# Plain queries for the first batch's scores, and its inter term summed on the output's bank

## The chip, the cores and the metric

One core of one Trainium2 chip. The metric is device time in microseconds (us). TensorE is called PE here, VectorE DVE, ScalarE ACT, GpSimd POOL, and SyncE SP; SP issues almost all the transfers. The kernel was timed three times before the change, and one further execution was profiled.

## The reference

Three layers run one after the other. The first is a retention layer with 8 heads of 64 features over 2 batches of 768 tokens. The two others are MLPs from 512 to 2048 and back, the first behind a Fourier mix. In float32:

```
for b in range(nb):                                   # blocks of 64 tokens
    intra = einsum('bhic,bhjc->bhij', qb, kb) * Dmask[None]
    intra = einsum('bhij,bhjd->bhid', intra, vb)
    inter = einsum('bhid,bhde->bhie', qb * lam_pow[None], kv_state)
    out[:, :, sl] = intra + inter
    kv_state = lam_block * kv_state + einsum('bhsd,bhse->bhde', kb * rev_pow, vb)
x = out as (batch, token, 512)
u = x + real(fft(fft(x, axis=1), axis=2))
u = u + relu(layernorm(u) @ w_ch1) @ w_ch2
out = u + relu((layernorm(u) * g_ln) @ w_ch1b) @ w_ch2b
```

The change concerns `intra` and `inter` only.

## The kernel before

The retention works on chunks of 128 tokens, six to a batch. For a chunk c the kernel computes masked scores, their product with v (the output O), and an inter term from the running state of the chunks before. Float32 data that goes through fast products is split into two float16 parts, high and low, and three of the four products are summed (`PASS`). So each score tile goes DVE (mask, L324), ACT (high part, L327), POOL (low part, L329), and then PE (O, L400). The scores and the inter term themselves are float32 products on PE; one such product stands as two records in the trace.

The two batches are treated differently. Batch 0 runs alone at the start and is followed by its Fourier mix. Batch 1 runs later, between the products of the first MLP, which by then has work for PE.

In batch 0 a score product uses all 128 rows of the PE array. Two heads lie on top of each other in the 128 partitions of the key tile; the queries are loaded into rooms that have been cleared (`qz`, L184 to L189), each head's half into columns of its own (L170), so that one product of 256 columns gives two heads. Plain queries (`qt`) are loaded as well for chunks 1 to 5. In batch 1 a score product uses 64 rows and 128 columns for one head, and the code writes the two halves of the array in turn, one head of the upper and one of the lower rows (L339 to L343).

The inter term of batch 0 multiplies the plain queries by a tile that holds the state of two heads on its diagonal (`diag`, L355). DVE scales the product by the decay of each token (`lp`, L359), and then DVE adds it to the output while it reads O out of its PSUM bank (L406; L404 for chunk 0, which has no inter term). The state goes POOL (decay, L425), PE (L432), DVE (add, L439), ACT (copy to `diag`, L444).

SP issues loads in the order of the code. What comes first is lambda, the loads of chunks 0 to 5 in turn, then the first weight tiles (`ws`, L252), the Fourier tables, more weight tiles, and the first two chunks of batch 1.

The order on the other engines is set in two ways. From the start to chunk 4's inter term, and again from the first MLP on, a planner at compile time lays out each engine's queue from its own estimates. Between the two, the string `ORDER` gives the order by hand: `s` is chunk 4's state, `O4` and `O5` the outputs, `B0` and `B1` the score tiles of chunk 5, `I` its inter term, `R`, `k` and `j` the folds that start the Fourier mix, `c` steps of the first weight conversions (L269 to L273 on DVE), `W12` twelve filler products on PE. The engines execute their queues in order, whichever way the order came about.

SBUF tiles of the retention come from a pool of 13 rooms (`f`), from 8 rooms for loads (`ld`), and from rooms that weights use later (`w1_*`, `w2_*`). PSUM banks come in groups `at` (3), `dn` (3) and `up` (2); batch 0's scores use `at`, its outputs and inter products `up`.

Of the kernel before, what the change touches and what calls it, by code (L numbers as in the profile page):

```python
# [43 lines left out]
c0 B1 B1 s B0 O4 B0 O4 B0 O4 c0 B1 s s c0 R k2 j2 s k2 c0 B0 I B1 c0 I k2 O5 O5 j2 c1 k2 O5 j2 k2 W12 d24 O5  # L44
# [69 lines left out]
def tile_retention_fourier_mlp(ctx: ExitStack, tc: tile.TileContext, a: dict, out: bass.AP):  # L114
# [49 lines left out]
    def load(b, c, names=("kt", "qt", "v", "k")):  # L164
        for nm in names:
            n = ("kt", "qt", "v", "k").index(nm)
            if b == 0 and nm == "qt":
                for e in range(2):
                    r = slice(e * D, (e + 1) * D)
                    sp.dma_start(qz[c % 4][r, :, e], a[nm][b, c, r].rearrange("p (i t) -> p i t", t=P))  # L170
                if c == 0:
                    continue
            if b == 0 and c >= 2:
                t = wpool.tile([P, 512], F32, tag=f"w2_{(4 * (c - 1) + n) % 16}", name=f"{nm}{b}_{c}")
            elif b == 0 and nm == "qt":
                t = f32t(f"qt{b}_{c}")
# [7 lines left out]
    qrooms = [wpool.tile([P, 2, 4, 512], F16, tag=f"w1_{g}", name=f"qz{g}").rearrange("p a k n -> p (a k n)").bitcast(F32)  # L184
              for g in range(2)]
    qz = [qrooms[c // 2][:, c % 2 * 1024:c % 2 * 1024 + 1024].rearrange("p (i e t) -> p i e t", e=2, t=P) for c in range(4)]
    for c in range(4):
        for e in range(2):
            (dve if c % 2 == 0 else pool).memset(qz[c][(1 - e) * D:(2 - e) * D, :, e], 0.0)  # L189
# [26 lines left out]
    diag = [diag[:, i * 512:(i + 1) * 512].rearrange("p (i n) -> p i n", n=P) for i in range(2)]  # L216
    for i in range(2):
        for e in range(2):
            pool.memset(diag[i][(1 - e) * D:(2 - e) * D, :, e * D:(e + 1) * D], 0.0)
# [93 lines left out]
    def attn_x(b, c, x, bk):  # L313
        if b == 0:
            pss[x] = bank(bk["s"], f"ps_s{b}_{c}_{x}")
            for i in range(2):
                pe.matmul(pss[x][:, i * 2 * P:(i + 1) * 2 * P], loaded["kt", b, c][:, (2 * x + i) * P:(2 * x + i + 1) * P],
                          qz[c % 4][:, 2 * x + i].rearrange("p e t -> p (e t)"), start=True, stop=True)
        yield
        m32 = f32t(f"m32_{b}_{c}_{x}")  # L320
        mk = mask[:, 4 * x:4 * x + 4] if b == 0 else mask[:, x::2]
        mk = mk[:, :, :P] if c >= 3 else mk[:, :, P:0:-1]
        mo, mi = (z.rearrange("p (h i) -> p h i", i=P) for z in (m32, pss[x]))
        dve.scalar_tensor_tensor(mo, mi, MS, mk, op0=ALU.mult, op1=ALU.mult)  # L324
        yield
        t = ms[b, c, x] = hl(f"m{b}_{c}_{x}")
# [5 lines left out]
    pss = {}  # L332

    def attn_b(b, c, bk):
        steps = [attn_x(b, c, x, bk) for x in range(2)]
# [12 lines left out]

    def attn_i_steps(b, c, bk):
        t = f32t(f"int{b}_{c}")  # L350
        lp_ = lp[:, 1 if c >= 3 else 0]
        if b == 0:
            ps = bank(bk["i"], f"ps_i{b}_{c}")
            for i in range(H // 2):
                pe.matmul(ps[:, i * P:(i + 1) * P], loaded["qt", b, c][:, i * P:(i + 1) * P], diag[(c - 1) % 2][:, i],  # L355
                          start=True, stop=True)
            yield
            to, ti = (z.rearrange("p (h d) -> p h d", h=H) for z in (t, ps))
            dve.tensor_tensor(to, ti, lp_.unsqueeze(2).to_broadcast([P, H, D]), op=ALU.mult)  # L359
        else:  # L360
            for e in range(2):
                ps, r = bank(bk["i"], f"ps_i{b}_{c}_{e}"), slice(e * D, (e + 1) * D)
                for i in range(H // 2):
                    cols = slice(i * D, (i + 1) * D)
                    pe.matmul(ps[:, cols], loaded["qt", b, c][r, i * P:(i + 1) * P], states[(c - 1) % 2][r, cols], start=True, stop=True)
                to = t.rearrange("p (i e d) -> p i e d", e=2, d=D)[:, :, e]
                ti = ps[:, :H // 2 * D].rearrange("p (i d) -> p i d", d=D)
                dve.tensor_tensor(to, ti, lp_[:, e::2].unsqueeze(2).to_broadcast([P, H // 2, D]), op=ALU.mult)
        xt[b, c] = t
        yield  # L370

    def attn_i(b, c, bk):
        if c > 0:
            run(attn_i_steps(b, c, bk))
# [19 lines left out]
    def attn_o_steps(b, c, bk):  # L394
        ps = bank(bk["o"], f"ps_o{b}_{c}")
        for h in range(H):
            (x, i), hc = divmod(h, 4) if b == 0 else (h % 2, h // 2), slice(h * D, (h + 1) * D)
            m_, mc = ms[b, c, x], slice(i * P, (i + 1) * P)
            for n, (x, y) in enumerate(PASS):
                pe.matmul(ps[:, hc], m_[:, x, mc], vs[b, c][:, y, hc], start=n == 0, stop=n == 2)  # L400
        yield
        x_ = U[b][c] if c < 3 else U[b][8 - c]
        if c == 0:
# [487 lines left out]
    def eng(n):  # L891
# [4 lines left out]
              "O5": lambda: attn_o_steps(0, 5, bk0), "I": lambda: attn_i_steps(0, 5, bk0), "R": lambda: row_fold(0)}  # L896
# [172 lines left out]
```

## Time and profile before

| | us |
|---|---|
| median of 3 runs | 640.51 |
| lowest, highest | 638.93, 642.65 |
| the profiled execution | 639.05 |
| its span, first to last instruction | 637.3 |

| engine | busy us (share of the span) | instructions |
|---|---|---|
| PE | 587.2 (92%) | 4645 |
| DVE | 466.4 (73%) | 988 |
| ACT | 260.1 (41%) | 524 |
| POOL | 296.8 (47%) | 307 |

Shares are means over stages with different limits, so the stages have to be read one by one. The mean granted clock of PE is 0.976 of full speed.

### The profile page before, as it was taken

The numbers are of one execution on the slowest core, as the hardware profiler recorded it, in microseconds if no ns is written. First come the engines' busy times: TensorE is split into PE (matmuls) and PEld (weight loads), VectorE is DVE, ScalarE is ACT, GpSimd is POOL, SyncE is SP. The second block draws the span as 40 slices with busy tenths as digits, with TensorE's granted clock in tenths as the row PEclk, the third lists the DMA queues.
The fourth block names the chain that finished last, engine by engine and source line by source line (L and its number), as shares of the span: only waits on it lengthen the run. The fifth ranks groups of instructions, "written<-read, shape, count | busy, mean of one in ns | idle before, by whom it ended". The sixth has DMA issues, their size and how long they took to land.

```text
span 637.3 us, 11878 instructions
## 1 busy us (share of the span) xinstructions
PE 587.2 (92%) x4645; PEld 386.3 (61%) x4645; DVE 466.4 (73%) x988; ACT 260.1 (41%) x524; POOL 296.8 (47%) x307
## 2 busy tenths in 40 slices
PE   5857969899999999889999986899999999999997
PEld 3753734556654455466777654665767676767773
DVE  6999797898698847975579999998653643464343
ACT  3643556664432342342228755565233213321110
POOL 6856748877546555651118986696211101120000
PEclk9969799799999999999999999999999999999999
DMA  9994126986300001011016743482010014102001
GB/s 247 304 382 162 43 68 163 241 264 209 100 1 1 1 18 34 0 26 26 2 34 182 195 138 102 149 203 62 17 51 17 17 57 61 34 2 72 29 1 49
DMA packets 47139, 59.96 MB, mean 94 GB/s; under 512 B 26095, under 2 KB 31084, under 8 KB 47084
## 3 DMA queue, kind: packets, MB, share of 16 engines
q1 hardware_dynamic: 46412, 59.13, 32.5%
q8 instruction: 36, 0.59, 0.4%
q10 hardware_dynamic: 672, 0.08, 0.1%
q14 instruction: 19, 0.16, 0.1%
HBM read 50.55 MB, written 4.72 MB: 87 GB/s over the span
## 4 chain that ended last, share of the span: by engine, by line
PE 55%; DVE 27%; DMA 8%; issue 4%; POOL 2%; ACT 2%; SPq 1%; DVEq 0%; ACTq 0%; POOLq 0%
PE ps_y L811 25%; PE ps L764 18%; PE ps_h L674 5%; DVE wf L273 3%; DVE ps_w L269 3%; DVE ps_w L271 3%; DMA kt<-in_kt 2%; DMA qz<-in_qt 2%; DVE bst L608 2%; PE ps_s L343 1%; DVE tr L727 1%; DMA ws<-in_w 1%; DVE wr L707 1%; DMA cdsd<-in_cd 1%; DVE h L797 1%
## 5 line engine op out<-in xcount | busy, mean ns | idle before, releaser
L811 PE MATMUL ps_y<-w,h 128*128 128x512 f16 x1152 | 281.0, 379 | 5.7 <-DVE h L797 2.4
L811 PEld LDWEIGHTS <-h 128*128 128x128 f16 x1152 | 109.1, 98 | 108.1 <-DVE h L797 5.0
L764 PEld LDWEIGHTS <-sw 128*128 128x128 f16 x1104 | 94.5, 98 | 22.5 <-issue 8.3
L286 POOL TENSOR_TENSOR w<-wf,w 128x512 f16<-128x512 f32 x64 | 76.2, 1196 | 50.4 <-ACT w L284 50.4
L764 PE MATMUL ps<-th,sw 128*128 128x192 f16 x828 | 92.8, 246 | 6.0 <-ACT th L739 3.0
L764 PEld LDWEIGHTS <-w 128*128 128x128 f16 x828 | 71.8, 98 | 20.1 <-issue 2.9
L674 PE MATMUL ps_h<-unT,w 128*128 128x384 f16 x396 | 76.1, 336 | 7.1 <-DVE h L689 3.6
L796 ACT ACTIVATE h<-ps 128x384 f16<-128x384 f32 x92 | 43.9, 489 | 78.8 <-DVE ps L790 67.5
L764 PE MATMUL ps<-unT,w 128*128 128x192 f16 x552 | 62.6, 246 | 0.0
L674 PEld LDWEIGHTS <-w 128*128 128x128 f16 x396 | 38.4, 100 | 38.7 <-issue 7.7
L784 DVE TENSOR_TENSOR t<-ps,s 128x192 f32<-128x192 f32 x46 | 16.2, 353 | 54.2 <-PE ps L764 54.1
L740 POOL TENSOR_TENSOR th<-ts,th 128x384 f16<-128x384 f32 x28 | 25.6, 931 | 62.3 <-ACT th L739 62.1
L797 DVE SCALAR_TENSOR_TENSOR h<-ps,h 128x384 f16<-128x384 f32 x92 | 49.1, 552 | 3.9 <-ACT h L796 2.3
L719 POOL TENSOR_TENSOR sw<-ws,sw 128x512 f16<-128x512 f32 x32 | 41.2, 1298 | 21.2 <-ACT sw L718 21.2
L637 POOL TENSOR_TENSOR uns<-un,uns 128x512 f16<-128x512 f32 x21 | 24.8, 1182 | 41.7 <-ACT uns L636 41.4
L283 ACT ACTIVATE wf<-wf 128x512 f32<-128x512 f32 x48 | 30.1, 629 | 33.2 <-DVE wf L273 32.9
L776 ACT COPY s<-ps 128x192 f32<-128x192 f32 x46 | 14.5, 317 | 70.4 <-PE ps L764 70.4
L269 DVE TENSOR_SCALAR ps_w<-ws 128x512 int32<-128x512 int32 x54 | 37.0, 688 | 7.0 <-DMA ws<-in_w 6.4
L284 ACT CAST w<-wf 128x512 f16<-128x512 f32 x64 | 39.0, 615 | 1.1
L790 DVE TENSOR_TENSOR ps<-ps,s 128x192 f32<-128x192 f32 x46 | 16.6, 362 | 29.4 <-PE ps L764 29.2
L616 POOL TENSOR_TENSOR rs<-rs,neghalf 128x1 f32<-128x1 f32 x24 | 13.7, 578 | 50.8 <-DVE rs L614 50.8
L271 DVE SCALAR_TENSOR_TENSOR ps_w<-ws,ps_w 128x512 int32<-128x512 int32 x54 | 37.0, 688 | 0.4
(154 smaller groups left out, 888.9 us busy)
## 6 DMA issues: line engine op xcount, KB each, us to landing
ws<-in_w SPq DMA_DIRECT2D x25, 512.0 KB, 4.8
ws<-in_w2b SPq DMA_DIRECT2D x16, 512.0 KB, 3.4
ws<-in_w1b SPq DMA_DIRECT2D x16, 512.0 KB, 3.9
kt<-in_kt SPq DMA_DIRECT2D x12, 256.0 KB, 3.7
v<-in_v SPq DMA_DIRECT2D x12, 256.0 KB, 5.6
k<-in_k SPq DMA_DIRECT2D x12, 256.0 KB, 5.2
qt<-in_qt SPq DMA_DIRECT2D x11, 256.0 KB, 5.9
pre<-in_w SPq DMA_DIRECT2D x4, 512.0 KB, 7.4
```

What stands on the lines that cost most here:

```text
L269: dve.tensor_scalar(part, raw[:, :, 1], 3, REST, op0=ALU.logical_shift_left, op1=ALU.bitwise_and)
L271: dve.scalar_tensor_tensor(part, raw[:, :, 1], KEEP, part, op0=ALU.bitwise_and, op1=ALU.bitwise_or)
L283: act.activation(t, t, AF.Copy, scale=sc)
L284: act.copy(hi, t)
L286: (dve if m == 0 and i in (LD1 if kind == 1 else LD2) else pool).tensor_tensor(lo, t, hi, op=ALU.subtract)
L674: pe.matmul(ps, w[:, i, k, fo:fo + P], x[:, j, k, :], start=n == 0, stop=n == 11)
L719: pool.tensor_tensor(lo, z, hi, op=ALU.subtract)
L740: pool.tensor_tensor(t[:, 1], z, t[:, 0], op=ALU.subtract)
L764: pe.matmul(ps, lhs, rhs, start=start and n == 0, stop=n == 5, skip_group_check=True)
L796: act.activation(hi, z, AF.Relu)
L797: dve.scalar_tensor_tensor(lo, z, 0.0, hi, op0=ALU.max, op1=ALU.subtract)
L811: pe.matmul(dn[blk][j], h[:, x, j * P:(j + 1) * P], w[:, y], start=f == 0 and n == 0, stop=f == NF - 1 and n == 2)
```

## The change

For batch 0 the cleared query rooms go, with their 8 memsets and 12 transfers. Plain queries are loaded for all six chunks. The scores of both batches come from one code: for each half e of the array's rows, four products of 64 rows and 128 columns, first all of e = 0, then all of e = 1. Batch 1's own loop, which put the halves in turn, goes too.

For the inter term of batch 0, the decay is laid out once in the layout of the queries (`lpt`: a broadcast copy on ACT, four transposes on PE and a scaled copy on ACT, for each of two token orders). POOL multiplies the queries of chunks 1 to 5 by it (`ql`). The four products of `ql` with `diag` follow O's 24 products on O's own bank. ACT reads that bank out for all six chunks; the DVE scaling (L359) and the DVE addition (L404, L406) go from batch 0. The two `I` leave `ORDER`. Batch 1's inter term stays as it is.

```
-c0 B1 B1 s B0 O4 B0 O4 B0 O4 c0 B1 s s c0 R k2 j2 s k2 c0 B0 I B1 c0 I k2 O5 O5 j2 c1 k2 O5 j2 k2 W12 d24 O5
+c0 B1 B1 s B0 O4 B0 O4 B0 O4 c0 B1 s s c0 R k2 j2 s k2 c0 B0 B1 c0 k2 O5 O5 j2 c1 k2 O5 j2 k2 W12 d24 O5
...
-            if b == 0 and nm == "qt":
-                for e in range(2):
-                    r = slice(e * D, (e + 1) * D)
-                    sp.dma_start(qz[c % 4][r, :, e], a[nm][b, c, r].rearrange("p (i t) -> p i t", t=P))
-                if c == 0:
-                    continue
...
-    for c in range(4):
-        for e in range(2):
-            (dve if c % 2 == 0 else pool).memset(qz[c][(1 - e) * D:(2 - e) * D, :, e], 0.0)
...
+    for i in range(2):
+        wide_lp, ps = f32t(f"lpw{i}"), bank("up", f"ps_lp{i}")
+        act.copy(wide_lp.rearrange("p (h d) -> p h d", h=H), lp[:, i].unsqueeze(2).to_broadcast([P, H, D]))
+        for k in range(NK):
+            pe.transpose(ps[:, k * P:(k + 1) * P], wide_lp[:, k * P:(k + 1) * P], ident)
+        act.activation(lpt[i], ps, AF.Copy, scale=1.0 / XS)
...
+        if b == 0 and c > 0:
+            xt[b, c] = f32t(f"ql{b}_{c}")
+            pool.tensor_tensor(xt[b, c], loaded["qt", b, c], lpt[1 if c >= 3 else 0], op=ALU.mult)
...
+    def attn_x(b, c, e, bk):
+        pss = bank(bk["s"], f"ps_s{b}_{c}_{e}")
+        for i in range(H // 2):
+            r, t = slice(e * D, (e + 1) * D), slice(i * P, (i + 1) * P)
+            pe.matmul(pss[:, t], loaded["kt", b, c][r, t], loaded["qt", b, c][r, t], start=True, stop=True)
+        yield
...
-        if b > 0:
-            for e in range(2):
-                pss[e] = bank(bk["s"], f"ps_s{b}_{c}_{e}")
-            for i in range(H // 2):
-                for e in range(2):
-                    r = slice(e * D, (e + 1) * D)
-                    t = slice(i * P, (i + 1) * P)
-                    pe.matmul(pss[e][:, t], loaded["kt", b, c][r, t], loaded["qt", b, c][r, t], start=True, stop=True)
+        for z in steps:
+            next(z)
...
-            dve.tensor_tensor(to, ti, lp_.unsqueeze(2).to_broadcast([P, H, D]), op=ALU.mult)
...
+        if b == 0 and c > 0:
+            for i in range(H // 2):
+                ic = slice(i * P, (i + 1) * P)
+                pe.matmul(ps[:, ic], xt[b, c][:, ic], diag[(c - 1) % 2][:, i], start=False, stop=True, skip_group_check=True)
         yield
         x_ = U[b][c] if c < 3 else U[b][8 - c]
-        if c == 0:
+        if b == 0:
+            act.activation(x_, ps, AF.Copy, scale=XS)
+        elif c == 0:
```

## Rows read from the trace of the kernel before

**Rows 1.** Stretch, length, busy (instructions) of PE, PEld, DVE, ACT, POOL, clock, DMA share, GB/s.

```profile
8.00:16.00 8.00, 6.73 (x57) 4.51 (x55) 4.10 (x7) 3.01 (x6) 4.82 (x4) 1.00 1.09 299
16.00:24.00 8.00, 6.88 (x99) 5.60 (x99) 6.98 (x11) 6.18 (x13) 5.90 (x6) 1.00 1.11 276
24.00:33.00 9.00, 8.09 (x104) 7.00 (x105) 8.02 (x12) 5.34 (x10) 8.23 (x9) 1.00 1.07 340
33.00:44.00 11.00, 5.88 (x89) 5.21 (x88) 10.69 (x12) 4.03 (x8) 6.57 (x8) 0.67 1.02 379
44.00:64.00 20.00, 15.41 (x84) 6.72 (x81) 20.00 (x36) 8.31 (x18) 11.79 (x11) 0.84 0.56 207
136.00:200.00 64.00, 63.56 (x586) 39.95 (x585) 55.39 (x94) 29.53 (x54) 42.19 (x40) 1.00 0.33 110
```

**Rows 2.** DVE's queue in order of time: start, us, instruction, idle before.

```profile
33.01 1.30 DVE L269 TENSOR_SCALAR wf<-ws 128x512 int32<-128x512 int32 x1 [0.99 <-DMA ws<-in_w]
...
35.44 0.68 DVE L359 TENSOR_TENSOR int<-ps_i,lp 128x512 f32<-128x512 f32 x1
36.03 1.27 DVE L324 SCALAR_TENSOR_TENSOR m<-ps_s,mask 128x512 f32<-128x512 f32 x2
...
40.16 3.50 DVE L273 SCALAR_TENSOR_TENSOR wf<-ws,wf 128x512 int32<-128x512 int32 x1
43.58 0.68 DVE L463 TENSOR_TENSOR e<-u 128x512 f32<-128x512 f32 x1
```

**Rows 3.** Groups by line, first 50 us: count, busy us, mean ns, idle before.

```profile
L317 PE MATMUL ps_s<-qz,kt 128*128 128x256 f32 x48 | 14.4, 435 | 8.1 <-DMA qz<-in_qt 7.5 <-DVE m L324 0.7
...
L298 POOL TENSOR_TENSOR kd<-k,rev 128x512 f32<-128x512 f32 x5 | 5.7, 1136 | 1.4 <-DMA k<-in_k 1.3
...
L302 ACT ACTIVATE vhl<-v 128x512 f16<-128x512 f32 x6 | 3.8, 627 | 3.8 <-DMA v<-in_v 3.8
...
L406 DVE SCALAR_TENSOR_TENSOR u<-ps_o,int 128x512 f32<-128x512 f32 x5 | 3.4, 679 | 0.3 <-PE ps_o L400 0.3
L359 DVE TENSOR_TENSOR int<-ps_i,lp 128x512 f32<-128x512 f32 x5 | 3.4, 675 | 0.0
```

**Rows 4.** Transfers issued in the first 34 us: count, KB each, us to landing.

```profile
qz<-in_qt SPq DMA_DIRECT2D x12, 128.0 KB, 6.4
...
qt<-in_qt SPq DMA_DIRECT2D x5, 256.0 KB, 5.4
```

**Rows 5.** POOL's queue in order of time.

```profile
8.04 1.04 POOL L298 TENSOR_TENSOR kd<-k,rev 128x512 f32<-128x512 f32 x1
10.32 1.16 POOL L329 TENSOR_TENSOR m<-m,m 128x512 f16<-128x512 f32 x1 [1.25 <-ACT m L327]
...
40.85 2.25 POOL L329 TENSOR_TENSOR m<-m,m 128x512 f16<-128x512 f32 x2
```

**Rows 6.** PE's queue in order of time, batch 0.

```profile
25.70 1.13 PE L317 MATMUL ps_s<-qz,kt 128*128 128x256 f32 x4
26.67 0.57 PE L400 MATMUL ps_o<-vhl,m 128*128 128x64 f16 x14
27.08 1.14 PE L355 MATMUL ps_i<-diag,qt 128*128 128x128 f32 x8
...
72.76 0.60 PE L649 MATMUL ps_l<-expo,un 128*128 128x128 f32 x4
```

**Rows 7.** PE's queue in order of time, batch 1.

```profile
137.78 1.71 PE L343 MATMUL ps_s<-qt,kt 64*128 64x128 f32 x16
...
148.80 1.16 PE L343 MATMUL ps_s<-qt,kt 64*128 64x128 f32 x8
...
161.49 1.17 PE L343 MATMUL ps_s<-qt,kt 64*128 64x128 f32 x16
162.59 1.47 PE L811 MATMUL ps_y<-w,h 128*128 128x512 f16 x6
163.99 1.10 PE L365 MATMUL ps_i<-state,qt 64*128 64x64 f32 x8
```

More of the change, by code (lines that the diff above doesn't have):

```diff
@@ L183, in tile_retention_fourier_mlp @@
     U = [[ut[b][:, j] for j in range(6)] for b in range(B)]
-    qrooms = [wpool.tile([P, 2, 4, 512], F16, tag=f"w1_{g}", name=f"qz{g}").rearrange("p a k n -> p (a k n)").bitcast(F32)
-              for g in range(2)]
-    qz = [qrooms[c // 2][:, c % 2 * 1024:c % 2 * 1024 + 1024].rearrange("p (i e t) -> p i e t", e=2, t=P) for c in range(4)]
-    for c in range(4):
-        for e in range(2):
-            (dve if c % 2 == 0 else pool).memset(qz[c][(1 - e) * D:(2 - e) * D, :, e], 0.0)
     load(0, 0, ("kt", "qt"))
@@ L216, in tile_retention_fourier_mlp @@
     diag = [diag[:, i * 512:(i + 1) * 512].rearrange("p (i n) -> p i n", n=P) for i in range(2)]
+    lpt = [z.rearrange("p a k n -> p (a k n)").bitcast(F32)[:, i * 512:(i + 1) * 512]
+           for z in (wpool.tile([P, 2, 4, 512], F16, tag="w1_1", name="lpt"),) for i in range(2)]
+    for i in range(2):
[4 more added lines that the diff above has]
+        act.activation(lpt[i], ps, AF.Copy, scale=1.0 / XS)
     for i in range(2):
@@ L311, in tile_retention_fourier_mlp @@
     PASS = ((0, 0), (0, 1), (1, 0))
[L313 to L318, printed above, removed]
+    def attn_x(b, c, e, bk):
[3 more added lines that the diff above has]
+            pe.matmul(pss[:, t], loaded["kt", b, c][r, t], loaded["qt", b, c][r, t], start=True, stop=True)
         yield
-        m32 = f32t(f"m32_{b}_{c}_{x}")
-        mk = mask[:, 4 * x:4 * x + 4] if b == 0 else mask[:, x::2]
+        m32 = f32t(f"m32_{b}_{c}_{e}")
+        mk = mask[:, e::2]
         mk = mk[:, :, :P] if c >= 3 else mk[:, :, P:0:-1]
-        mo, mi = (z.rearrange("p (h i) -> p h i", i=P) for z in (m32, pss[x]))
+        mo, mi = (z.rearrange("p (h i) -> p h i", i=P) for z in (m32, pss))
         dve.scalar_tensor_tensor(mo, mi, MS, mk, op0=ALU.mult, op1=ALU.mult)
         yield
-        t = ms[b, c, x] = hl(f"m{b}_{c}_{x}")
+        t = ms[b, c, e] = hl(f"m{b}_{c}_{e}")
         act.copy(t[:, 0], m32)
@@ L330, in attn_x @@
         yield
-    pss = {}
     def attn_b(b, c, bk):
-        steps = [attn_x(b, c, x, bk) for x in range(2)]
-        if b > 0:
-            for e in range(2):
-                pss[e] = bank(bk["s"], f"ps_s{b}_{c}_{e}")
-            for i in range(H // 2):
-                for e in range(2):
-                    r = slice(e * D, (e + 1) * D)
-                    t = slice(i * P, (i + 1) * P)
-                    pe.matmul(pss[e][:, t], loaded["kt", b, c][r, t], loaded["qt", b, c][r, t], start=True, stop=True)
+        steps = [attn_x(b, c, e, bk) for e in range(2)]
+        for z in steps:
+            next(z)
         for z in steps:
@@ L351, in attn_i_steps @@
         lp_ = lp[:, 1 if c >= 3 else 0]
-        if b == 0:
-            ps = bank(bk["i"], f"ps_i{b}_{c}")
+        for e in range(2):
+            ps, r = bank(bk["i"], f"ps_i{b}_{c}_{e}"), slice(e * D, (e + 1) * D)
             for i in range(H // 2):
[L355 to L358, printed above, removed]
-            dve.tensor_tensor(to, ti, lp_.unsqueeze(2).to_broadcast([P, H, D]), op=ALU.mult)
[L360 to L368, printed above, removed]
+                cols = slice(i * D, (i + 1) * D)
+                pe.matmul(ps[:, cols], loaded["qt", b, c][r, i * P:(i + 1) * P], states[(c - 1) % 2][r, cols], start=True, stop=True)
+            to = t.rearrange("p (i e d) -> p i e d", e=2, d=D)[:, :, e]
+            ti = ps[:, :H // 2 * D].rearrange("p (i d) -> p i d", d=D)
+            dve.tensor_tensor(to, ti, lp_[:, e::2].unsqueeze(2).to_broadcast([P, H // 2, D]), op=ALU.mult)
         xt[b, c] = t
@@ L372, in attn_i @@
     def attn_i(b, c, bk):
-        if c > 0:
+        if b > 0 and c > 0:
             run(attn_i_steps(b, c, bk))
@@ L396, in attn_o_steps @@
         for h in range(H):
-            (x, i), hc = divmod(h, 4) if b == 0 else (h % 2, h // 2), slice(h * D, (h + 1) * D)
-            m_, mc = ms[b, c, x], slice(i * P, (i + 1) * P)
+            (i, e), hc = divmod(h, 2), slice(h * D, (h + 1) * D)
+            m_, mc = ms[b, c, e], slice(i * P, (i + 1) * P)
             for n, (x, y) in enumerate(PASS):
-                pe.matmul(ps[:, hc], m_[:, x, mc], vs[b, c][:, y, hc], start=n == 0, stop=n == 2)
+                pe.matmul(ps[:, hc], m_[:, x, mc], vs[b, c][:, y, hc], start=n == 0 and (b > 0 or h == 0), stop=n == 2, skip_group_check=b == 0)
+        if b == 0 and c > 0:
+            for i in range(H // 2):
+                ic = slice(i * P, (i + 1) * P)
+                pe.matmul(ps[:, ic], xt[b, c][:, ic], diag[(c - 1) % 2][:, i], start=False, stop=True, skip_group_check=True)
         yield
         x_ = U[b][c] if c < 3 else U[b][8 - c]
-        if c == 0:
+        if b == 0:
+            act.activation(x_, ps, AF.Copy, scale=XS)
+        elif c == 0:
             dve.tensor_scalar(x_, ps, XS, None, op0=ALU.mult)
```

4 lines of the change are left out of this document (1 added, 3 removed).

## The prediction, made before the changed kernel was run

> **What bounds the kernel now.** I read the busy time by stretch first [rows 1], then the queues of DVE, POOL and PE through batch 0 [rows 2, 5, 6], the groups by line [rows 3], the transfers [rows 4], and last PE's queue where batch 1 is worked on [rows 7].
>
> The change touches two places with different limits. In the first, from 8 to 64 us, no engine holds alone from the start. From 8 to 16 us DVE works 4.10 and POOL 4.82 of 8 us with the DMA engines full, so the loads set the pace. From 16 to 33 us DVE works 15.00 of 17 us, POOL 14.13, and PE 14.97; three engines are within a tenth of each other, so taking work off one of them uncovers the next. From 33 to 44 us DVE has 10.69 of 11 and from 44 to 64 all 20.00 of 20 [rows 1]. There the order is written by hand and DVE is the bound, with conversion steps between the folds. In the second place, 136 to 200 us, PE works 63.56 of 64 us: whatever PE gets there in addition moves the end by as much.
>
> **The change part by part.**
>
> *Transfers.* Twelve transfers of 128 KB go (1,536 KB) and one of 256 KB comes [rows 4], so 1,280 KB or 1.31 MB less. At the 276 to 340 GB/s of the stretches from 16 to 33 us [rows 1] that is 3.9 to 4.7 us of transfer, and everything behind chunk 5 on SP lands about 4 us sooner. Only what waits for it gains. That is DVE's 0.99 us before the first conversion at 33.01 [rows 2], POOL's 1.4 us before three `kd` (L298), and a part of PE's 7.5 us before L317 [rows 3]. These waits lie in different engines' queues, and I count them inside the shift that POOL allows below.
>
> *DVE.* Five L359 and six read-outs (five L406, one L404 of the same size) go, at 0.68 us each [rows 3]. They start 0.59 us apart (35.44 to 36.03) [rows 2], so 11 x 0.59 = 6.5 us of DVE's queue. Two of them, the scaling and the read-out of chunk 5, lie in the stretch from 44 to 64 us where DVE has no gap: 1.2 us, which I count in full. The other nine (5.3 us) stand ahead of the first fold at 43.58 [rows 2]. Together with the 0.99 us wait that is 6.3 us by which the fold could come sooner. The lower bound is a gain of nothing, if DVE waits for POOL there instead.
>
> *POOL.* Five products of 128x512 come. Their price is that of L298, the same shape: 1.14 us in the mean [rows 3], so 5.7 us; 5.2 us if all take the 1.04 us of the one at 8.04 [rows 5]. Four memsets at the very start go and are worth nothing, since they end before POOL has its first data. From 8.04 until the last two score tiles end at 43.10 (40.85 + 2.25) [rows 5], POOL is busy for about 25.5 of 35 us [rows 1]: 4.82 to 16 us, 5.90 to 24, 8.23 to 33 and about 6.5 in the rest. Between 16 and 33 us it has 2.9 us free, and three of the five new products (3.4 us) fall there. It is full there from now on. The two for chunks 1 and 2 find room before 16 us, where 3.2 us are free. Queued behind each `ql` are `dec` (the state waits for it) and the low parts of the scores (O waits for them). Counting POOL without a gap from its first score tile at 10.32 [rows 5]: 25.5 us of work, less 1.04 for the first `kd`, plus 5.7, give 30.2 us and an end at 40.5. With the 1.2 us of gaps that a queue in order will still have, the end is at 41.8 instead of 43.10, so 1.3 us sooner. This is what I take for the shift of the hand-ordered part. DVE could give 6.3; but its step at 40.16, a conversion with two SBUF inputs, took 3.50 us and ended 0.56 us after POOL's two score tiles did [rows 2, 5], so the first fold stood behind POOL's work as well.
>
> Of this last row the Trainium skill says in GPSIMD Engine Reference (section Specifications) that POOL's SBUF interface is shared with VectorE, against DVE instructions with two SBUF inputs among others. By that rule each `ql` would also stretch a DVE step, while the removed DVE steps, which read PSUM and one SBUF tile, never were stretched; the sum would lose up to 5.7 us more. The trace agrees in kind: 0.675 and 0.679 us in the mean for the removed ones, against 3.50 for that conversion.
>
> *ACT.* Six read-outs and, at the start, four passes come, ten at 0.63 us (L302) [rows 3]. ACT has 3.7 us free from 24 to 33 us and more elsewhere [rows 1]. The read-outs stand behind mask casts on ACT; if that cover were gone, O's bank would come free up to 0.6 us later per chunk. The four passes at the start stand ahead of chunk 0's casts, in the stretch paced by loads; nothing, or 1.3 us if two of them delay the first cast.
>
> *PE in batch 0.* A chunk's scores were two runs of 0.97 us (25.70 to 26.67) [rows 6] and become two of eight records in 64 rows. Such a run has 1.16 us, of which 0.07 lies under the next instruction (162.59 + 1.47 against 163.99) [rows 7], so 1.09. Twelve runs cost 12 x 0.12 = 1.4 us more. The inter products stay at eight records per chunk (1.14 us, L355), and eight transposes come (four took 0.60, L649) [rows 6], in the stretch paced by loads. PE was busy 6.88 of 8 and 8.09 of 9 us [rows 1], so 1.4 us spread over six chunks still fits. In chunk 5 the products with `diag` now stand behind O's, and delay that read-out by about 1.1 us, 2 at the clock of 0.67. DVE reaches chunk 5's folds only several steps later, so nothing.
>
> Where PE changes between 128 and 64 rows, the overlap with the next instruction is 0.07 us (163.99), against 0.16 between full-width runs (26.67 + 0.57 against 27.08) [rows 6, 7]: 0.09 us a change. TensorEngine Tiling (Array Packing), section Key Properties, of the Trainium skill says that changing the tiling mode drains the engine. By that rule the whole overlap goes, 24 x 0.16 = 3.8 us; by the rows 24 x 0.09 = 2.2 us, of which the 1.09 above holds half.
>
> *PE in batch 1.* Here the halves of the array no longer alternate. Where they did, sixteen records took 1.17 us (161.49); where the planner had placed one half alone, eight took 1.16 us (148.80) [rows 7]. A chunk of the new form costs 2.2 us. I found two of the six chunks in halves, two in turn, one between (1.71 us), and one at half clock which I leave out. So the loss is 1.1 + 1.1 + 0.6 = 2.8 us, in the stretch where PE has no gap [rows 1], and all of it is on the path. The bounds are 0 (the planner alternates anyway) and 6 x 1.1 = 6.6.
>
> **Sum.** -1.2 (DVE, 44 to 64 us) - 1.3 (hand-ordered part starts sooner) + 2.8 (batch 1) = +0.3 us. On the profiled execution's 639.05 that is 639.4. The median of the runs is 640.51, 1.46 above it, so 640.8 stands for a median: no change that can be told. About 0.5% (3.2 us) is what a measurement of this kernel can tell.
>
> **The rivals.**
>
> *Batch 0's relief comes through whole (faster).* POOL's new products find gaps, and DVE reaches the first fold 5.3 + 0.99 us sooner: 640.5 - 1.2 - 6.3 + 2.8 = 635.8. For it: POOL has 9.5 us of gaps in 35, loads come 4 us sooner, and DVE is full from 33 to 64 us. Against it: 14.13 of 17 us on POOL from 16 to 33 us.
>
> *POOL becomes the bound (slower).* The planner puts each `ql` ahead of the score tiles that are due, since it belongs to a chunk's first task, and POOL's gaps stay where they are. Then 3 to 5.7 us of the new work lengthen POOL's chain to the last score tile. It decides once less than half of the 5.7 us falls into gaps. Price: 640.5 - 1.2 + 3 + 2.8 = 645.1, and 647.8 with all of it. For it: the 3.50 us step. Against: loads that come sooner.
>
> *The array's mode changes cost their whole overlap.* PE, at nine tenths between 16 and 33 us, gets 1.4 + 1.7 us more and becomes the bound: 640.8 + 3.1 = 643.9. The rows show 0.09 of 0.16 us a change, so little speaks for it. The Trainium skill's rule on draining, above, is this rival's.
>
> *Batch 1 loses nothing.* The planner alternates the halves although the code doesn't: 640.8 - 2.8 = 638.0. Two split chunks in the trace show that it moves single products; but it took one half first there, not both in turn.
>
> **How the numbers follow.** Forecast 0.42 (637.5 to 644); relief whole 0.24; POOL the bound 0.24; mode changes 0.05; batch 1 unharmed 0.05. Faster: 0.85 of 0.24, a tenth of 0.42 and some of the last, 0.27. Slower: 0.85 of 0.24, a sixth of 0.42 and half of 0.05, 0.30. The rest, 0.43, is no change. The range reaches to 634.5 and to 648, beyond both large rivals by what runs differ; the forecast's own is 637.5 to 644.
>
> **What would show it.** POOL from 16 to 33 us at 16 of 17 us or more, and its last score tile of batch 0 near 41.8 us. The first fold on DVE near 42 us; at 37 the first rival holds, at 46 the second. `ws` landing near 29 us. In batch 1, score runs of sixteen records near 2.2 us, with PE without gaps. Wrong would be: scores of batch 1 still at 1.2 us, or a stretch after 200 us that differs by over 2 us, since nothing there is changed and the planner alone would have moved it.

## The result, and the profile after

The change made the kernel slower. Its median of four runs is 648.88 us (647.56 to 650.96), against 640.26 us (638.93 to 642.65, four runs) before: a ratio of 1.0131 [1.0099, 1.0163], or about 8.4 us. The profiled execution took 650.96 us with a span of 649.2, the longest of the four; the profiled one of before took 639.05 with 637.3.

Three marks in PE's queue cut the 11.9 us between the two spans. The first product of the first MLP starts at 80.40 instead of 74.29: +6.1. From there to the last inter products of batch 1 it takes 115.67 instead of 111.83 us: +3.8. The rest has 453.13 instead of 451.18: +2.0. The marks, before and then changed:

```profile
74.29 0.85 PE L664 MATMUL ps_h<-unT,w 128*128 128x128 f16 x12
...
186.12 1.60 PE L365 MATMUL ps_i<-state,qt 64*128 64x64 f32 x16
...
80.40 0.85 PE L649 MATMUL ps_h<-unT,w 128*128 128x128 f16 x12
...
196.07 1.60 PE L344 MATMUL ps_i<-state,qt 64*128 64x64 f32 x16
```

Such a mark is one execution's. In a kernel whose batch 0 is that of before (halves apart, below) the first one stands at 75.79, so a shift of 1.5 us by itself says nothing.

Busy time by stretch of the changed kernel, columns as in [rows 1]:

```profile
8.00:16.00 8.00, 8.00 (x53) 6.78 (x54) 5.96 (x7) 5.25 (x10) 6.12 (x6) 1.00 1.05 389
16.00:24.00 8.00, 8.00 (x87) 7.21 (x83) 4.02 (x7) 3.91 (x9) 6.48 (x7) 1.00 1.05 396
24.00:33.00 9.00, 8.22 (x93) 7.10 (x92) 3.51 (x6) 2.22 (x4) 7.93 (x8) 1.00 1.03 398
33.00:44.00 11.00, 9.99 (x103) 8.86 (x100) 6.18 (x11) 6.91 (x14) 7.30 (x7) 1.00 0.93 354
44.00:64.00 20.00, 14.11 (x133) 9.10 (x133) 16.95 (x31) 9.28 (x20) 12.86 (x15) 0.91 0.09 28
136.00:200.00 64.00, 63.97 (x620) 40.97 (x617) 54.21 (x92) 30.75 (x58) 43.05 (x42) 1.00 0.42 139
```

The reader is to see that from 8 to 44 us PE has become the busy engine: 34.21 of 36 us, where it had 27.58 [rows 1]. DVE has fallen from 29.79 to 19.67 us, so its work did go, and it idles. POOL has gaps. The loads run at 389 to 398 GB/s instead of 276 to 340. The clock column says 1.00, and PE's queue shows that this is not so. Columns: start, us, instructions.

```profile
17.75 2.07 PE L314 MATMUL ps_s<-qt,kt 64*128 64x128 f32 x8
...
29.89 2.07 PE L314 MATMUL ps_s<-qt,kt 64*128 64x128 f32 x8
31.90 1.30 PE L379 MATMUL ps_o<-vhl,m 128*128 128x64 f16 x21
33.01 2.06 PE L383 MATMUL ps_o<-diag,ql 128*128 128x128 f32 x8
...
37.23 1.14 PE L383 MATMUL ps_o<-diag,ql 128*128 128x128 f32 x8
38.30 1.16 PE L314 MATMUL ps_s<-qt,kt 64*128 64x128 f32 x8
39.39 0.23 PE L379 MATMUL ps_o<-vhl,m 128*128 128x64 f16 x2
...
51.12 2.06 PE L383 MATMUL ps_o<-diag,ql 128*128 128x128 f32 x8
...
127.19 2.41 PE L314 MATMUL ps_s<-qt,kt 64*128 64x128 f32 x16 [2.23 <-DVE wf L267]
...
158.41 1.71 PE L314 MATMUL ps_s<-qt,kt 64*128 64x128 f32 x16
```

The same eight score records take 2.07 us up to 32 us and 1.16 from 38 us on; the same eight inter records take 2.06 at 33.01 and 1.14 at 37.23. So PE ran at the lower of its two clock levels (1.2 GHz) until about 36 us and at the upper one (2.4 GHz) after. In the kernel before, full-width scores were at full speed by 10.4 us, four records in 1.10 us where the first eight had taken 3.58:

```profile
6.20 3.58 PE L317 MATMUL ps_s<-qz,kt 128*128 128x256 f32 x8 [6.20 <-DMA qz<-in_qt]
10.39 1.10 PE L317 MATMUL ps_s<-qz,kt 128*128 128x256 f32 x4 [0.61 <-DMA qz<-in_qt]
```

In these traces the clock column holds 1.00 until the first change that was recorded, and ahead of that the durations are what counts. The Trainium skill warns that clock events in traces have been seen to be unreliable (TensorE: Matmul & The Clock Gate, Part 1); this trace agrees, with 1.00 in the column beside 2.07 us.

Groups by line in the first 50 us, columns as in [rows 3]:

```profile
L314 PE MATMUL ps_s<-qt,kt 64*128 64x128 f32 x96 | 20.8, 406 | 7.5 <-DMA qt<-in_qt 6.8 <-DVE m L320 0.8
...
L320 DVE SCALAR_TENSOR_TENSOR m<-ps_s,mask 128x512 f32<-128x512 f32 x12 | 8.1, 685 | 10.3 <-PE ps_o L379 8.5 <-PE ps_st L417 1.5 <-PE ps_o L383 0.3
...
L296 POOL TENSOR_TENSOR ql<-qt,lpt 128x512 f32<-128x512 f32 x5 | 6.8, 1360 | 3.7 <-PE ps_o L379 3.7
```

The scores of batch 0 take 20.8 us, against 14.4 for L317 in [rows 3]. DVE waited 10.3 us ahead of its masks, all of it for PE, and POOL 3.7 us ahead of a `ql`, for PE as well. DVE's queue, columns as in [rows 2]:

```profile
28.65 0.42 DVE L263 TENSOR_SCALAR wf<-ws 128x512 int32<-128x512 int32 x1
33.24 0.69 DVE L320 SCALAR_TENSOR_TENSOR m<-ps_s,mask 128x512 f32<-128x512 f32 x1 [4.17 <-PE ps_o L379]
...
42.72 1.29 DVE L320 SCALAR_TENSOR_TENSOR m<-ps_s,mask 128x512 f32<-128x512 f32 x2 [2.93 <-PE ps_o L379]
...
47.59 1.45 DVE L448 TENSOR_TENSOR e<-u 128x512 f32<-128x512 f32 x1
48.97 1.64 DVE L448 TENSOR_TENSOR o<-u 128x512 f32<-128x512 f32 x1
50.53 1.37 DVE L450 TENSOR_TENSOR e<-e 128x255 f32<-128x255 f32 x1
...
54.65 0.76 DVE L448 TENSOR_TENSOR e<-u 128x512 f32<-128x512 f32 x1 [1.14 <-ACT u L399]
...
69.12 2.40 DVE L493 SCALAR_TENSOR_TENSOR cst<-ps_d,cst 128x384 f16<-128x384 f32 x5
```

The first fold is 4.0 us later than the 43.58 of [rows 2]. From it to the transforms' sums (`cst`, 69.12 here, 63.02 before) it takes 21.53 us instead of 19.44, so 2.1 more: that makes the 6.1.

POOL's last score tiles now run beside these folds:

```profile
47.13 2.94 POOL L325 TENSOR_TENSOR m<-m,m 128x512 f16<-128x512 f32 x2 [0.30 <-ACT m L323]
```

### The profile page after: what moved, and what is told of

It is laid out like the page before. It is cut to its first block, busy times and chain, and to the rows that moved or that the text cites. A ratio compares the mean times of both kernels' runs of the same rounds, so it can differ in the third digit from the quotient of the medians.

```text
span 649.2 us, 11961 instructions
## 1 busy us (share of the span) xinstructions
PE 600.5 (93%) x4701; PEld 399.3 (62%) x4701; DVE 455.1 (70%) x973; ACT 263.7 (41%) x534; POOL 302.6 (47%) x308
## 4 chain that ended last, share of the span: by engine, by line
PE 64%; DVE 22%; issue 4%; POOL 3%; ACT 3%; DMA 2%; SPq 0%; DVEq 0%; POOLq 0%; ACTq 0%
PE ps_y L796 28%; PE ps L749 20%; PE ps_h L659 5%; PE ps_s L314 4%; DVE wf L267 3%; DVE ps_w L263 2%; DVE ps_w L265 2%; DMA ws<-in_w 2%; DVE tr L712 2%; DVE wr L692 1%; PE ps_o L379 1%; DVE bst L593 1%; PE ps_d L481 1%; POOL m L325 1%; DVE ws L697 1%
## 5 line engine op out<-in xcount | busy, mean ns | idle before, releaser
L796 PEld LDWEIGHTS <-h 128*128 128x128 f16 x1152 | 110.4, 98 | 113.6 <-issue 8.5
L314 PE MATMUL ps_s<-qt,kt 64*128 64x128 f32 x192 | 32.9, 350 | 9.9 <-DMA qt<-in_qt 6.8
L762 DVE TENSOR_TENSOR s<-ps,s 128x192 f32<-128x192 f32 x46 | 16.2, 352 | 30.1 <-ACT s L761 30.1
```

The costliest lines, as they stand in the source:

```text
L314: pe.matmul(pss[:, t], loaded["kt", b, c][r, t], loaded["qt", b, c][r, t], start=True, stop=True)
L796: pe.matmul(dn[blk][j], h[:, x, j * P:(j + 1) * P], w[:, y], start=f == 0 and n == 0, stop=f == NF - 1 and n == 2)
```

## The experiments

Three questions were asked: is it PE's clock or POOL that sets batch 0's new length, what do the halves of batch 1 cost, and what is the change worth without both. The parts first.

**Scores alone.** The kernel before, with the clearing and `qz` taken out and plain scores of 64 rows in batch 0; L359, L406 and the separate inter products stay.

```
-            for i in range(2):
-                pe.matmul(pss[x][:, i * 2 * P:(i + 1) * 2 * P], loaded["kt", b, c][:, (2 * x + i) * P:(2 * x + i + 1) * P],
-                          qz[c % 4][:, 2 * x + i].rearrange("p e t -> p (e t)"), start=True, stop=True)
+            for i in range(H // 2):
+                r, t = slice(x * D, (x + 1) * D), slice(i * P, (i + 1) * P)
+                pe.matmul(pss[x][:, t], loaded["kt", b, c][r, t], loaded["qt", b, c][r, t], start=True, stop=True)
```

> The kernel before with the score part alone: plain queries and 64-row score products in batch 0; the inter term stays with DVE, batch 1 keeps its halves in turn. Theory A (in batch 0 the 64-row products leave PE at its lower clock, and PE is then the bound): 8 score records take about 2.07 us until 30 us or later as in the changed kernel, the first product of the first MLP starts near 80 us instead of 74.3, time 644 to 648. Theory B (the new POOL products and the order around them are the cause): clock up near 10 us, first MLP product within 1 us of 74.3, time 639 to 642.

Measured: 641.36 us, ratio 1.0014 [0.9986, 1.0042]. PE's queue there:

```profile
20.62 2.08 PE L341 MATMUL ps_i<-diag,qt 128*128 128x128 f32 x8
...
24.37 1.62 PE L341 MATMUL ps_i<-diag,qt 128*128 128x128 f32 x8
...
30.27 1.16 PE L341 MATMUL ps_i<-diag,qt 128*128 128x128 f32 x8
```

The lower clock is there as well (2.08 us for eight records), but it ends near 25 us, within the second run of full-width float32 products, the first of which stands at 20.62. In the changed kernel these products stand behind O's, the first at 33.01, and the clock rises after them. The first MLP starts at 73.25, and the time is level with before: 64-row scores with a rise near 25 us cost nothing that can be told. Neither theory came whole: the low clock was there, as A said, and the time was B's. The trace is of the shortest of ten runs (638.52 to 647.36).

**Inter term alone.** Full-width scores from `qz` stay; `lpt`, `ql`, products on O's bank and ACT's read-out as in the change.

```
-        if c > 0:
+        if b > 0 and c > 0:
             run(attn_i_steps(b, c, bk))
...
+            pool.tensor_tensor(xt[b, c], loaded["qt", b, c], lpt[1 if c >= 3 else 0], op=ALU.mult)
...
+                pe.matmul(ps[:, ic], xt[b, c][:, ic], diag[(c - 1) % 2][:, i], start=False, stop=True, skip_group_check=True)
...
+            act.activation(x_, ps, AF.Copy, scale=XS)
```

> The kernel before with the inter part alone: scaled queries on POOL, products on the output's bank, ACT reads it out, no I in ORDER; batch 0's scores stay full-width from cleared rooms, batch 1 keeps its halves in turn. Theory A: the clock rises near 10 us as in the kernel before, first MLP product between 71 and 75 us, time 636 to 641. Theory B: the last score tile of batch 0 on POOL ends near 49 us instead of 43, first MLP product near 79 us, time 644 to 648.

Measured: 644.66 us, 1.0044 [1.0027, 1.006]. Busy time by stretch:

```profile
24.00:33.00 9.00, 6.96 (x74) 5.34 (x74) 6.57 (x10) 4.99 (x10) 9.00 (x8) 1.00 1.08 327
33.00:44.00 11.00, 6.98 (x110) 6.01 (x110) 7.38 (x10) 6.49 (x13) 9.99 (x12) 1.00 1.03 399
```

With PE at full speed (it has gaps of 2 and 4 us) POOL is the full engine. So the rival on POOL describes this part on its own; but the first MLP starts at 75.27, only 1.0 us late. The other 2.7 us of this execution lie in batch 1, whose code is that of before: PE waits 0.64 us there ahead of 143.90, the clock is 0.79 of full speed from there to 152 us, and sixteen inter records take 2.20 us instead of 1.60. So not all of this kernel's loss is POOL's.

**Halves apart, in the kernel before.** Only batch 1's loop is turned round.

```
-            for i in range(H // 2):
-                for e in range(2):
+            for e in range(2):
+                for i in range(H // 2):
```

> The kernel before with one change in batch 1: the score products of one half of the array after those of the other, not in turn. Theory C (lost overlap of the halves costs PE 2.8 us in a stretch without gaps): sixteen records near 2.2 us in every chunk, 642.5 to 643.5. Rival (the planner's order, or gaps, absorb it): within 1 us of the kernel before.

Measured: 643.07 us, 1.0027 [1.0004, 1.005], so 0.3 to 3.2 us. From the first MLP's first product to batch 1's last inter products it takes 116.22 instead of 111.83 us in the profiled execution. But at the upper clock no run of sixteen records takes 2.2 us: the planner mixed the halves, and the two chunks that took 1.17 us in turn take about 1.71. That is 1.1 us for all of batch 1, so the 2.8 of theory C is not borne out by PE's own price, and where the rest of the 4.4 us of this execution comes from was not traced.

**Fillers first.** The changed kernel with twelve full-width products on PE ahead of the scores (1.45 to 6.75 us), while it waits for the first loads. Only `NW` differs, one of the constants that L53 sets together.

```
-NW = 0
+NW = 12
```

> The changed kernel with twelve filler products of 128 rows and 512 columns on PE ahead of the first load's arrival. Theory A1 (64-row products do not hold the higher clock): the clock rises near 6 us, and within some us of the first scores 8 records are back at 2.07 us; time within 2 us of the changed kernel's 648.9. Rival A2 (the clock only had to be raised once): 8 records stay at 1.16 us through batch 0, first MLP product near 74 us, time 641 to 644.

Measured: 643.47 us, 1.003 [1.0008, 1.0053]; 5.4 us less than the changed kernel. PE's queue, then the busy time:

```profile
9.36 1.16 PE L314 MATMUL ps_s<-qt,kt 64*128 64x128 f32 x8
...
18.77 2.04 PE L314 MATMUL ps_s<-qt,kt 64*128 64x128 f32 x8 [1.27 <-DVE m L320]
```

```profile
16.00:24.00 8.00, 6.48 (x73) 5.51 (x67) 6.25 (x7) 4.14 (x8) 8.00 (x8) 0.56 1.05 397
24.00:33.00 9.00, 8.14 (x96) 7.27 (x93) 5.49 (x9) 4.34 (x8) 8.81 (x8) 0.63 1.03 395
33.00:44.00 11.00, 8.71 (x135) 7.60 (x129) 7.11 (x10) 7.96 (x17) 9.71 (x12) 1.00 0.97 364
```

The clock is up at the start and falls near 17 us, after PE has had gaps (1.37 us ahead of 15.58); it is up again near 30.6, after full-width inter products at 28.87. PE now has gaps and POOL has none from 16 to 24 us. The first MLP starts at 74.98. The time is the rival's, but the clock did not stay up. The fillers also made the planner lay out another order in batch 0, so this pair alone does not part the clock from the order.

**One half by itself.** PE alone in a kernel that does nothing else of the layers: bursts of 120 float32 records each, on one half, on the halves in turn, on all rows, and on one half right behind that.

```
+    ps = burst("one", 60, (up,), x)
+    y = idle("two", ps, 2)
+    ps = burst("two", 60, (up, lo), y)
+    y = idle("full", ps, 2)
+    ps = burst("full", 60, (both,), y)
+    ps = burst("again", 60, (lo,), y)
```

> PE alone, none of the layers: four bursts of 60 float32 products of 128 columns each, on plain data. One half of the array's rows; then, after an idle stretch, the two halves in turn; after another idle stretch, all 128 rows; and at once behind it one half again. Theory A (64-row products of one half do not raise the clock): the first burst stays at 0.26 us a record for all of its 31 us, the third starts there and goes to 0.12 after some us, the fourth goes back to 0.26 within its length. Rival (it is not the 64 rows, but what stands between them in the kernel, or the start of a program): the first burst rises to 0.13 after some us as the third does.

```profile
3.44 25.97 PE L35 MATMUL ps_one<-x 64*128 64x128 f32 x120 [3.44 <-DMA x<-in_w]
47.67 9.66 PE L35 MATMUL ps_two<-x_two 64*128 64x128 f32 x120 [18.26 <-DVE x_two L43]
75.62 16.06 PE L35 MATMUL ps_full<-x_full 128*128 128x128 f32 x120 [18.28 <-DVE x_full L43]
91.61 13.66 PE L35 MATMUL ps_again<-x_full 64*128 64x128 f32 x120
```

One half alone took 25.97 us, 0.216 us a record from the first to the last: the clock never rose. With the halves in turn, and on all rows, records start slow and end at about half that time (the full-width ones at 0.112), so there it rose. Right behind, at the upper level, one half ran 13.66 us at 0.114 a record and kept it. So one half did not raise the clock here in 26 us, though it held it for 13.7, where theory A had it fall back. This is one execution, and the burst on one half is also the first of its program; but the start of a program does not by itself keep the clock down, since it rose by 10.4 us in the kernel before. The Trainium skill says that the lower clock is the default and that activity of TensorE releases it (TensorE: Matmul & The Clock Gate, Part 1). By that sentence the new score runs would have released it as the old ones did, and the changed kernel would not have stayed at the lower level until 36 us; the first burst shows otherwise, and the measurement decides.

**Turns again in batch 1.** The changed kernel, batch 1's scores from a loop in turn.

```
+        if b > 0:
...
+            for i in range(H // 2):
+                for e in range(2):
+                    score(b, c, e, i, both[e])
```

> The changed kernel with batch 1's halves in turn again as before; batch 0 as changed. Theory C (the lost overlap is on PE's path): 646.5 to 647.5 beside the changed kernel's 648.9, two chunks of batch 1 at 1.2 us for sixteen records. Rival (absorbed): within 1 us of 648.9.

Measured: 647.5 us, 1.0098 [1.0068, 1.0128], so 1.4 us less than the changed kernel by the medians and 2.1 by the ratios, whose intervals overlap. The time is theory C's, the mark is not: no chunk's sixteen records take 1.2 us, as the planner mixed the halves again (1.82 and 1.49 us, or two runs of 1.16). Of the 3.6 us between the two profiled executions 1.0 lies between the first MLP's start and batch 1's last inter products, and 2.5 behind them.

**Queries on DVE.** Fillers first, and `ql` on DVE instead of POOL: were POOL the bound behind the clock, this should free it.

```
-            pool.tensor_tensor(xt[b, c], loaded["qt", b, c], lpt[1 if c >= 3 else 0], op=ALU.mult)
+            dve.tensor_tensor(xt[b, c], loaded["qt", b, c], lpt[1 if c >= 3 else 0], op=ALU.mult)
```

> The changed kernel with the twelve fillers at the start, and the five query products on DVE instead of POOL. Theory P (in the stretch from 16 to 44 us POOL is the bound once the clock is up, and its last score tile decides): that tile ends 3 us or more before the 45.1 us of the run with fillers alone, first product of the first MLP at 72 to 74 us, 640 to 642. Rival (the output's longer way over PE and ACT decides, whatever POOL does): within 1 us of the run with fillers alone, 643.5.

Measured: 648.83 us, 1.0144 [1.0105, 1.0182]: as slow as the change, a miss.

```profile
24.00:33.00 9.00, 9.00 (x94) 7.63 (x92) 8.76 (x10) 3.94 (x8) 5.69 (x5) 0.50 1.03 395
33.00:44.00 11.00, 10.37 (x96) 9.12 (x94) 4.72 (x9) 5.28 (x10) 5.49 (x8) 0.66 0.93 356
```

POOL is idle for almost half the time, and the clock, which fell near 13 us after a gap of 0.43 us on PE, stays at its lower level until about 40: PE is full, and the first MLP starts at 81.48. A kernel with POOL relieved is as slow as the changed one when PE is at its lower clock. What POOL costs at the upper one, the question of theory P, this run does not tell.

**Fillers in the kernel before.**

```
-NW = 0
+NW = 12
```

> The kernel before with the twelve fillers at the start and nothing else. Theory A says that the clock costs only where PE is the bound: in the kernel before it rises near 10 us by itself and loads and DVE set the pace, so within 1 us of 640.9. Rival (the fillers give a gain of their own, so that what they gave the changed kernel is no evidence on its 64-row products): 636 to 638.

Measured: 640.46 us, 1.0012 [0.9989, 1.0034]. The fillers by themselves are worth nothing that can be told.

**Fillers with the scores alone.** The first experiment's kernel with the same edit of `NW`.

> The kernel before with plain queries and 64-row scores in batch 0, inter term as before, and the twelve fillers. Without fillers it was level with the kernel before (1.0014). If what it lost on PE's clock until 24 us was on the path, and its sooner loads are a gain: 637 to 639, faster than both kernels. If DVE's hand-ordered stretch decides: 640 to 642.

Measured: 647.29 us, 1.0094 [1.0063, 1.0124]; a miss, and the most telling one.

```profile
24.00:33.00 9.00, 9.00 (x78) 7.92 (x77) 6.95 (x11) 4.98 (x10) 7.43 (x7) 0.50 1.04 398
33.00:44.00 11.00, 11.00 (x70) 10.18 (x71) 5.20 (x9) 2.49 (x5) 4.62 (x4) 0.50 0.92 351
```

Here the fillers brought the clock up early, it fell between 10 and 11 us, after PE had waited 0.93 us for queries, was up again from about 20 to 24 us, and was low from 24 to 44 us, where the kernel without fillers had it up. The first MLP starts at 82.00 instead of 73.25. There is no `ql` and no product on O's bank in this kernel, and it is 5.9 us slower by the medians (5.1 by the ratios) than the one without fillers. The two differ in twelve products before 7 us and in the order that the planner laid out after them. The ten runs of this kernel, which have one order, part the two: a lower mean granted clock goes with a longer run (correlation -0.95), from 640.75 us at 0.976 to 650.11 at 0.950. So with one program the time goes with the clock, though a mean over the whole run does not say in which stretch, and it is not so in every kernel (0.02 for fillers with turns in both batches, below).

Three full-width inter runs pass in the low stretch without raising the clock, the first and the last of them:

```profile
24.35 2.06 PE L341 MATMUL ps_i<-diag,qt 128*128 128x128 f32 x8
...
39.74 2.06 PE L341 MATMUL ps_i<-diag,qt 128*128 128x128 f32 x8
```

**Halves in turn in both batches**, in an order tied product by product, without and with fillers.

```
+                with tc.issue_after(last) if last is not None else nullcontext():
+                    last = score(b, c, e, i, both[e])
```

> The changed kernel with the halves of the array in turn in both batches (chunk 5 of batch 0 excepted), the order of the score products tied. No fillers. Theory A' (one half alone does not raise the clock but the halves in turn do, as the second burst did): the clock rises before 20 us, at least 10 us sooner than the changed kernel's 36; first product of the first MLP at 74 to 77 us; 641 to 644. Rival (the products around the scores keep it down, however the halves stand): 646.5 to 648, as with batch 1's halves in turn alone, 647.5.

> The changed kernel with fillers and with the halves in turn in both batches. Theory A' with PE at its higher clock for most of batch 0: 638 to 641, POOL then the fullest engine from 16 to 44 us. Rival: no better than fillers and batch 1's turns, 641.5 to 643.

Measured: 647.14 us, 1.0101 [1.0064, 1.0137] without, and 644.09, 1.0059 [1.0031, 1.0087] with fillers. In the profiled execution without fillers (642.95, the shortest of its runs) the clock rose at about 10.6 us, as the bursts had it, but was down again from about 18 to 28 us, and once more from 36; its runs spread from 642.95 to 649.99. So turns raise the clock and do not keep it up, and the expected gain did not come. The tied order also moves other products, and no run separates that from the turns.

**Fillers and turns in batch 1 together.** The changed kernel with fillers first and batch 1 in turn.

> The changed kernel with the twelve fillers at the start and batch 1's halves in turn, batch 0's scores as changed. If the two causes add (fillers gave 648.9 to 643.5, batch 1's turns 648.9 to 647.5): 641.5 to 642.5, within 0.3% of the kernel before. If they overlap: 643 to 644.

Measured: 640.1 us, 0.9994 [0.9968, 1.002]: level with the kernel before, and below the 641.5 to 642.5 that was expected if the two gains add. Its twelve runs, of one order, go with the clock too (correlation -0.93): 638.01 us at 0.979, 643.10 at 0.957 and 644.48 at 0.959.

```profile
16.00:24.00 8.00, 7.03 (x79) 6.06 (x73) 6.30 (x7) 4.10 (x8) 8.00 (x8) 0.50 1.05 399
24.00:33.00 9.00, 8.15 (x95) 7.30 (x95) 5.44 (x8) 4.33 (x8) 8.91 (x8) 0.65 1.03 395
33.00:44.00 11.00, 8.51 (x125) 7.45 (x125) 7.14 (x11) 7.97 (x16) 9.73 (x12) 1.00 0.98 363
```

POOL has 26.64 of 28 us, the first fold is at 42.39 and the first MLP at 74.79. Even here the clock is low from 13 to about 30 us, and PE has gaps in that stretch, 0.97 of 8 us and 0.85 of 9. The score runs of batch 1 are not shorter than with fillers alone, 11.74 against 11.58 us in all, since the planner mixed the halves in both. Of the 3.8 us between these two profiled executions, 1.0 lies between the first MLP's start and batch 1's last inter products and 2.65 behind them, in another order of the planner's. So what this edit gives back is not shown to be the halves' overlap.

Start of the first MLP and the stretches behind it, in the profiled executions (us). The three add up to the span of that one execution, which need not be near the median: for scores alone and for turns in both batches it was the shortest run.

| kernel | median | first MLP product | from there to batch 1's last inter products | rest |
|---|---|---|---|---|
| before | 640.26 | 74.29 | 111.83 | 451.18 |
| changed | 648.88 | 80.40 | 115.67 | 453.13 |
| scores alone | 641.36 | 73.25 | 111.56 | 451.89 |
| scores alone, fillers | 647.29 | 82.00 | 112.11 | 451.29 |
| inter alone | 644.66 | 75.27 | 114.54 | 451.79 |
| halves apart alone | 643.07 | 75.79 | 116.22 | 450.89 |
| changed, fillers | 643.47 | 74.98 | 113.88 | 453.24 |
| changed, turns in batch 1 | 647.5 | 80.25 | 114.68 | 450.67 |
| changed, fillers, turns in batch 1 | 640.1 | 74.79 | 112.92 | 450.59 |
| changed, fillers, queries on DVE | 648.83 | 81.48 | 117.56 | 447.66 |
| before, fillers | 640.46 | 75.38 | 111.55 | 450.77 |
| changed, turns in both | 647.14 | 75.28 | 114.17 | 451.75 |
| changed, fillers, turns in both | 644.09 | 75.49 | 112.92 | 453.69 |

## Why the prediction was wrong, point by point

**The step that failed** is PE in batch 0: "PE was busy 6.88 of 8 and 8.09 of 9 us [rows 1], so 1.4 us spread over six chunks still fits." It took the 1.16 us of a 64-row run from batch 1, where PE runs at its upper clock, and put it into a stretch where, in the changed kernel, the clock was still at its lower level. Scores cost 6.4 us more (20.8 against 14.4), not 1.4, and the other products of that stretch slowed with them (21 products of O took 1.30 us at 31.90; 19 took 0.73 later). PE then had no gap to hide it in: it was busy 8.00 of 8 us from 8 to 16 and from 16 to 24 us. Why the clock stayed down is in part argued. One part is shown, in one burst: scores of one half did not raise it. The other fits the trace and is not shown: inter products moved behind O, so that the full-width float32 work after which the clock rose starts at 33.01, against 20.62 with scores alone; in the kernel with scores alone and fillers, three such runs raised nothing. That the clock costs the time rests on three things: the equal runs of 2.07 and 1.16 us on a PE without gaps, the ten runs of one program that go with the clock, and two pairs with and without fillers, -5.4 us with the change and +5.9 us with scores alone, each time as the clock in the trace went, though the planner's order differs within each pair.

**Changes between 64 and 128 rows: right.** At 38.30 the run of 1.16 us overlaps the next instruction by 0.07 us, as the rows of before had it; the rival that priced the whole overlap has nothing for it.

**Transfers: right.** In the first 34 us seven loads of 256 KB stand for queries, six for batch 0 and the first of batch 1, which SP issues at 31.57 instead of 40.47:

```profile
qt<-in_qt SPq DMA_DIRECT2D x7, 256.0 KB, 5.4
```

The first conversion on `ws` ran at 28.65 without a wait, where 29 was expected for the landing. Nothing came of it, since PE was late.

**DVE: the work went, the gain did not.** The first fold came at 47.59 where 42 was expected. The mark set for the POOL rival, 46, was passed for another reason: POOL itself waited 3.70 us for PE. With fillers and turns the first fold is at 42.39, close to the 42 of the forecast; but in the kernel with halves apart, whose batch 0 is that of before, it is at 40.11, so this mark does not decide.

**POOL: full as said, and mis-sized.** In the changed kernel POOL has 14.41 of 17 us from 16 to 33 us, since it waits for PE. With fillers and turns it has 16.91, as the prediction had it. But the gain of "1.3 (hand-ordered part starts sooner)" does not come: POOL's last score tile there ends at 44.94, not at 41.8, and later than the 43.10 of before. Its prices were too low. `ql` took 1.36 us in the changed kernel and 1.63 there, not 1.14, and the twelve score tiles took 16.1 us there, against 14.7 before.

**44 to 64 us: 1.2 us counted as a gain, 2.1 lost.** Three folds beside POOL's last score tiles and its next product took 4.46 us, where the same ones took 1.77 in the kernel before, in a gap of POOL (43.10 to 45.05). In that kernel the slow step stood ahead of the first fold instead, the conversion of 3.50 us at 40.16, and with halves apart, on the same batch 0, it is a fold beside POOL's two score tiles:

```profile
40.71 4.69 DVE L463 TENSOR_TENSOR o<-u 128x512 f32<-128x512 f32 x1
```

There the stretch from the first fold to `cst` is 23.09 us, longer than in the changed kernel, so part of the 2.1 us is only where this one slow step falls. And the sentence on chunk 5, "DVE reaches chunk 5's folds only several steps later, so nothing", failed: a fold at 54.65 waits 1.14 us for a row that ACT copies out of chunk 5's output (read out at 53.21, behind the inter products of 51.12, at 2.06 us). With fillers and turns the stretch is 21.60 us, so this part does not go with the fillers. The Trainium skill's rule on the SBUF interfaces that POOL shares with VectorE (GPSIMD Engine Reference, Specifications), which the prediction weighed against `ql`, fits these folds of two SBUF tiles; the traces agree, 0.68 us in a gap of POOL against 1.45 to 4.69 beside its tiles, but no run here took POOL away and left the rest, so this cause is argued, not shown.

**Batch 1: a loss, but not by the step that was counted.** 2.8 us were counted, at 2.2 us for each chunk that was not in halves before. At the upper clock no run of sixteen records took that: the planner mixed the halves and left 1.71 (158.41), and the 2.41 at 127.19 stands where the clock falls. Leaving out the chunk that ran at a lower clock, as the prediction did, the score runs of batch 1 take 9.77 us instead of 8.69, so 1.1 more. Halves apart alone cost 0.3 to 3.2 us. Turning them back in the changed kernel gave 1.4 us, and with fillers 3.4 (643.47 to 640.1; 2.3 by the ratios), of which only 1.0 each lies ahead of batch 1's last inter products. That the halves' overlap is worth 2.8 us is not shown.

**After 200 us: at the bound.** The rest differs by 2.0 us in the changed kernel, and by 2.1 with fillers, where over 2 was given as a sign of being wrong. The planner did lay out another order there: PE waits 1.93 us ahead of batch 1's first transforms, where it waited 1.19 before and 0.66 with fillers and turns in batch 1.

**The account.** Fillers take off 5.4 us (6.5 by the ratios) and turns in batch 1 another 3.4 (2.3), together 8.8 of a loss of 8.4 to 8.6. The first part goes with PE's clock in batch 0. The second is what an edit of batch 1 gave, mostly behind batch 1, and its cause is open. What the lighter DVE and the earlier loads bring is spent by then: net nothing, where +0.3 less the 2.8 of batch 1 had promised a gain of 2.5. That POOL's dearer products and the later folds are what spends it fits the traces and is not shown by an edit.

**Open.** Why the clock rises when it does, after inter products at 28.87 or 33.01 and not after those at 24.35 to 39.74 in another kernel, was not settled. Nor was why it falls between 10 and 18 us in the kernels with fillers, while one half held it for 13.7 us in the bursts: PE had gaps there and changes between kinds of products, and no run separates the two. No kernel was tried that keeps the clock up throughout batch 0. No kernel here beats the one before by more than the measurement can tell.

## What to carry to other kernels

Take a product's price from a stretch with the same clock, and ask whether the new products would raise that clock: compare the durations of equal runs early and late in the trace, not the clock column alone. Work that looks redundant (zeros in half of the rows) can be what keeps PE fast, and moving products can move the rise. When one engine's relief is large, see which engine is full once that relief is granted: here, with PE's delay gone, it was POOL. And where a planner lays out the queues, an edit in one place can move the order far behind it, so compare the orders before a gain is put down to the edit.

## What was not expected of the hardware

- In the bursts, float32 products on 64 of 128 rows ran 25.97 us without a pause at 0.216 us a record; on 128 rows they ended at 0.112, and halves in turn took 9.66 us for the same 120 records.
- The same products on one half, right behind full-width ones, kept 0.114 us a record for 13.66 us.
- In the changed kernel the profile's clock column showed 1.00 up to 44 us, though equal runs took 2.07 us up to 32 us and 1.16 from 38 us on.
- The runs of one kernel (scores alone, with fillers) lay between 640.75 us at a mean granted clock of 0.976 and 650.11 at 0.950.
